# Block-sorted attention and a two-layer network on one core: a key load issued earlier, a product piece one slot earlier, and five products of zeros

## Chip, cores and metric

One core of a Trainium2 chip (trn2). The metric is the device time of the whole program in microseconds, lower is better. Each execution carries a state: "slow" ones (a few per cent longer, of any version: 237.31 us beside 233.39 to 233.86 in the first four runs of the kernel before) are left out of every comparison here unless the text says so.

## The reference, cut to what matters

```python
# q, k, v: (4 batches, 8 heads, 768 positions, 64); sort_net: (4, 8, 8, 8)
P = sort_net                                    # five rounds of exp, row and column normalisation
k_sorted = einsum('bhij,bhjcd->bhicd', P, k_b)  # blocks of 96 positions mixed by P
v_sorted = einsum('bhij,bhjcd->bhicd', P, v_b)
attn = softmax(q_b @ k_sb.T / 8)                # within each block
x = (attn @ v_sb), heads side by side           # (3072, 512)
h = x @ w_in                                    # (3072, 2048)
out = (s * relu(h)**2 + b) @ w_out              # (3072, 512)
```

## The kernel before

The work is cut into eight half batches, t = 0 to 7. The dense network of one half batch (`ffn1`, `ffn2`) carries pieces of the next attention between its products, through a queue of slots. Four places matter here.

The pieces that mix keys and values with P. Their results go to tiles in PSUM and are copied from there (`ks<-tk`, 0.42 to 0.81 us each at the start, on VectorE or ScalarE). A key piece multiplies 128 neighbouring numbers of `kb` as weights; a v piece of batch 0 takes its weights one number in 64:

```python
def k_piece(b, c0, nc2, nb, eng):
    ...                                          # ps: a PSUM tile, psa (3 buffers) or psb (2)
    for c in range(nc2):
        nc.tensor.matmul(out=ps[:, c, :],
                         lhsT=kb[pr, c0 + 2*c:c0 + 2*c + 2, :].rearrange("p c d -> p (c d)"),
                         rhs=rhs, start=True, stop=True)
    ...                                          # four copies to ks, on VectorE or ScalarE
def v_piece0(d0, n, eng):
    for t in range(n):
        nc.tensor.matmul(out=ps[:, t, :], lhsT=vb[0:64, :, d0 + t], rhs=..., start=True, stop=True)
    evac(VS[0][:, :, d0:d0 + n], ps[0:BLK].rearrange("p t g -> p g t"), eng)
```

The start, in TensorE's order. `warm_up` is a run of products of zeros, put there for the clock alone. In the profile of before each of them takes 421 ns at first and 272 from about 6.3 us on; what the eight later ones are worth is measured under no_pwarm:

```python
warm_up(76)
build_pd1()
q_half(0, "s")
k_piece(0, 0, 16, 1, "v")();  k_piece(0, 32, 16, 1, "s")()
k_piece(0, 64, 8, 1, "v")();  k_piece(0, 80, 8, 1, "s")()
v_piece0(0, 16, "v");  v_piece0(16, 16, "s");  v_piece0(32, 16, "v")
s_piece(0, 0);  v_piece0(48, 8, "v");  s_piece(0, 1);  v_piece0(56, 8, "v")
s_piece(0, 2);  s_piece(0, 3)
for hp in range(NHP):
    p_piece(0, hp, 0, 2)
    ...
    warm_up(2, psa)
```

GpSimd's queue, which issues the loads and also sums w_out for the bias, and the queue of pieces in which batch 2's keys are first used (K key pieces, V2 v pieces, S2 scores, P2 attention products, T transposes, `nothing` an empty slot):

```python
csums(0, 8)
v_read(1, nc.sync)            # batch 1's v comes back from DRAM, where v_piece1 wrote it
ffn1(1, ...)
load_v(*brows(3))
csums(8, NF)
qu = Queue([..., seq(lambda: load_q(2), lambda: load_k(*brows(2)), bias_piece),
            V2[0], S2(2, 0), ..., V2[5],
            seq(T(2), S2(3, 0), K(2, 0, 16, "s")), nothing, P2(3, 0),
            seq(S2(3, 2), K(2, 32, 16, "s")), nothing, P2(3, 2), ...], 24)
ffn2(0, qu); ffn2(1, qu)
```

The softmax here doesn't subtract the row's maximum and nothing guards it: scores larger than these inputs give would overflow.

Of the kernel before, what the change touches and what calls it, by code (L numbers as in the profile page):

```python
# [18 lines left out]
def kernel(  # L19
# [12 lines left out]
    nc = tc.nc  # L32
# [45 lines left out]
    def load_q(b, part=slice(0, 128)):  # L78


        if b > 1:
            qr[b] = qrp.tile([128, TQ, H, D], BF, tag="qr", name=f"qr{b}")
            for t in range(TQ):
                nc.gpsimd.dma_start(  # L84
                    out=qr[b][:, t],
                    in_=q[b][:, t * 128:(t + 1) * 128, :].rearrange("h p d -> p h d"))
            return
        if b not in qr:
            qr[b] = qrp.tile([128, H, TQ, D], BF, tag="qr", name=f"qr{b}")
        nc.gpsimd.dma_start(  # L90
            out=qr[b][part].rearrange("p h t d -> p h (t d)"),
            in_=q[b].rearrange("h (p t) d -> p h (t d)", t=TQ)[part])

    def load_k(rows, prow, n=1):
        for c0 in range(0, BLK, BLK // n):
            cs = slice(c0, c0 + BLK // n)
            nc.gpsimd.dma_start(out=kb[prow, cs, :], in_=kraw[rows, cs, :])

    def load_v(rows, prow):
        nc.gpsimd.dma_start(out=vb[prow, 0:BLK, :], in_=vraw[rows])  # L100

    def brows(b):
        return slice(b * 64, (b + 1) * 64), slice((b % 2) * 64, (b % 2) * 64 + 64)
# [6 lines left out]
    zt = const.tile([128, 256], BF)  # L110
# [41 lines left out]
    for c0 in range(0, d_ff, FCH):  # L152
        w = const.tile([128, NHP, FCH], BF, name=f"wi{c0}")
        nc.gpsimd.dma_start(
            out=w, in_=moe_w_in.rearrange("(hp p) f -> p hp f", p=128)[:, :, c0:c0 + FCH])
# [5 lines left out]
    for f0 in range(0, NF, FW):  # L161
        w = const.tile([128, FW, d_model], BF, name=f"wo{f0}")
        nc.gpsimd.dma_start(
            out=w, in_=moe_w_out.rearrange("(f p) n -> p f n", p=128)[:, f0:f0 + FW, :])
# [8 lines left out]
    def wo_at(f):  # L173
        return wos[f // FW][:, f % FW, :]
# [61 lines left out]
    def evac(out, in_, eng):  # L236
        if eng == "v":
            nc.vector.tensor_copy(out=out, in_=in_)  # L238
        else:
            nc.scalar.copy(out=out, in_=in_)  # L240
# [38 lines left out]
            nc.sync.dma_start(out=QT[b][:, :, t * 128:(t + 1) * 128],  # L279
                              in_=qr[b][:, t].rearrange("p h d -> p (h d)"), transpose=True)  # L280

    def k_piece(b, c0, nc2, nb, eng):




        pr = brows(b)[1] if nb == 1 else slice(0, 128)
        rhs = (pd1[pr] if b < 2 else pd2[pr, b - 2]).rearrange("p e m i -> p (e m i)")
        if nc2 * nb > 8:
            ps = psa.tile([128, nc2, nb * 64], FP, tag="a", name="tk")  # L290
        else:
            ps = psb.tile([128, nc2, nb * 64], FP, tag="b", name="tk")
        for c in range(nc2):
            nc.tensor.matmul(out=ps[:, c, :],  # L294
                             lhsT=kb[pr, c0 + 2 * c:c0 + 2 * c + 2, :].rearrange("p c d -> p (c d)"),
                             rhs=rhs, start=True, stop=True)
        g0 = (b % 2) * 32

        def half(cp):
            if b == 0:  # L300
                cs = slice(c0 + cp, c0 + 2 * nc2, 2)
            else:
                cs = slice(cp * (BLK // 2) + c0 // 2, cp * (BLK // 2) + c0 // 2 + nc2)
            for e in range(2):
                evac(ks[e * 64:(e + 1) * 64, g0:g0 + nb * 32, cs].rearrange(
                         "p (b g) c -> p b g c", b=nb),
                     ps[cp * 64:(cp + 1) * 64].rearrange(
                         "p c (b e g) -> p e b g c", b=nb, e=2)[:, e], eng)

        half(0)  # L310
        return lambda: half(1)

    def v_piece0(d0, n, eng):

        if n > 8:
            ps = psa.tile([128, n, 64], FP, tag="a", name="tv")
        else:
            ps = psb.tile([128, n, 64], FP, tag="b", name="tv")
        for t in range(n):
            nc.tensor.matmul(out=ps[:, t, :], lhsT=vb[0:64, :, d0 + t],  # L320
                             rhs=pd1[0:64].rearrange("p e m i -> p (e m i)"),
                             start=True, stop=True)
        evac(VS[0][:, :, d0:d0 + n], ps[0:BLK].rearrange("p t g -> p g t"), eng)
# [42 lines left out]
    def s_piece(t, hp):  # L366

        b, half = divmod(t, 2)
        g0 = (b % 2) * 32 + hp * NB + half * HB
        sc = psa.tile([BLK, 2, 512], FP, tag="a", name="sc")  # L370
        for n in range(HB):
            for e in range(2):
                pr = slice(e * 64, (e + 1) * 64)
                q0 = (half * HB + n) * BLK
                nc.tensor.matmul(out=sc[:, e, n * BLK:(n + 1) * BLK], lhsT=ks[pr, g0 + n, :],  # L375
                                 rhs=QT[b][pr, hp, q0:q0 + BLK], start=True, stop=True)
        at = atp.tile([BLK, 2, TG], BF, tag="at", name="at")
        nc.scalar.activation(out=at, in_=sc[:, :, 0:TG], func=AF.Exp, scale=scale)  # L378
        AT[t, hp] = at

    def p_piece(t, hp, n0=0, nn=HB):

        b, half = divmod(t, 2)
        at = AT[t, hp]
        if t not in X:
            X[t] = xp.tile([BLK, HB, d_model], BF, tag="x", name="x")
        x = X[t]
        atf = at.rearrange("p e t -> p (e t)")
        if nn < HB:
            p1 = psb.tile([128, 512], FP, tag="b", name="pv")  # L390
            pv = [p1[:, e * nn * VW:(e + 1) * nn * VW] for e in range(2)]
            pvv = p1[0:BLK, 0:2 * nn * VW].rearrange("p (e n w) -> p e n w", e=2, w=VW)
        else:
            p2 = psa.tile([128, 2, 512], FP, tag="a", name="pv")
            pv = [p2[:, 0], p2[:, 1]]
            pvv = p2[0:BLK, :, 0:nn * VW].rearrange("p e (n w) -> p e n w", w=VW)
        for e in range(2):
            for n in range(n0, n0 + nn):
                c0 = (e * HB + n) * BLK
                m = 128 if c0 + 128 <= 2 * TG else BLK  # L400
                gi = e * 32 + hp * NB + half * HB + n
                nc.tensor.matmul(out=pv[e][0:m, (n - n0) * VW:(n - n0 + 1) * VW],  # L402
                                 lhsT=atf[:, c0:c0 + m],
                                 rhs=VS[b][:, gi, :], start=True, stop=True)
        rec = rtp.tile([BLK, 2, HB], FP, tag="rec", name="rec")
        nc.vector.reciprocal(out=rec[:, :, 0:nn], in_=pvv[:, :, :, D])  # L406
        nc.vector.tensor_tensor(  # L407
            out=x[:, n0:n0 + nn, hp * 128:(hp + 1) * 128].rearrange("p n (e d) -> p e n d", e=2),
            in0=pvv[:, :, :, 0:D],
            in1=rec[:, :, 0:nn].unsqueeze(3).broadcast_to([BLK, 2, nn, D]), op=ALU.mult)  # L410
# [62 lines left out]
    def x_turn(t):  # L473

        XT[t] = xtp.tile([128, HB * NHP, BLK], BF, tag="xt", name="xt")
        nc.sync.dma_start(out=XT[t], in_=X[t].rearrange("p n m -> p (n m)"), transpose=True)
# [99 lines left out]
    def seq(*fs):  # L576
        def run():
            for f in fs:
                f()
        return run  # L580

    def S2(t, hp):
        return lambda: (s_piece(t, hp), s_piece(t, hp + 1))

    def P2(t, hp):
        return lambda: (p_piece(t, hp), p_piece(t, hp + 1))

    def T(t):
        return lambda: x_turn(t)
# [32 lines left out]
    build_pd1()  # L622
    q_half(0, "s")
    k_piece(0, 0, 16, 1, "v")()
    k_piece(0, 32, 16, 1, "s")()
    k_piece(0, 64, 8, 1, "v")()
    k_piece(0, 80, 8, 1, "s")()
    v_piece0(0, 16, "v")
    v_piece0(16, 16, "s")
    v_piece0(32, 16, "v")  # L630
    s_piece(0, 0)
    v_piece0(48, 8, "v")
# [36 lines left out]
    def csums(f0, f1):  # L669
        for f in range(f0, f1):  # L670
            if f == 1:
                nc.gpsimd.tensor_tensor(out=csum, in0=wo_at(0), in1=wo_at(1), op=ALU.add)
            elif f > 1:
                nc.gpsimd.tensor_tensor(out=csum, in0=csum, in1=wo_at(f), op=ALU.add)  # L674
# [2 lines left out]
    v_read(1, nc.sync)  # L677
    ffn1(1, Queue([nothing] * 4 + [build_pd2] + [nothing] * 3, 8))
    load_v(*brows(3))
    csums(8, NF)  # L680

    def K(b, c0, nc2, eng):
        return lambda: k_piece(b, c0, nc2, 1, eng)()
# [1 line left out]
    V2 = [lambda c0=c0: v_piece2(c0, "s") for c0 in range(0, BLK, 16)]  # L685
    qu = Queue([nothing, seq(lambda: q_piece(1, 2, "s"), K(1, 0, 16, "v")), nothing,
                seq(K(1, 32, 16, "s"), K(1, 64, 16, "v")), nothing,
                seq(lambda: load_q(2), lambda: load_k(*brows(2)), bias_piece),
                V2[0], S2(2, 0), V2[1], S2(2, 2), V2[2], V2[3], P2(2, 0), V2[4], P2(2, 2), V2[5],
                seq(T(2), S2(3, 0), K(2, 0, 16, "s")), nothing, P2(3, 0),  # L690
                seq(S2(3, 2), K(2, 32, 16, "s")), nothing, P2(3, 2),
                seq(T(3), lambda: q_turn(2)), K(2, 64, 16, "s")], 24)
    ffn2(0, qu)
# [56 lines left out]
```

## Time and profile before

| | before |
|---|---|
| time, median of 3 | 233.86 us (233.76 to 237.31) |
| span of the profiled run | 231.2 us |
| TensorE busy | 222.2 us, 96% |
| half clock in the profiled run | 16.56 to 26.80 us |
| first product of the first layer (hps) | 26.84 us |
| first score piece of t = 3 (sc) | 80.56 us |
| first product of the layer for t = 2 (hps) | 92.40 us |

The granted clock is the share of TensorE's full clock that the profile records; half clock is 0.50. It lasted 10.24 us in this profile and 13.65 in that of the changed kernel, three and four times 3.41; I call 3.41 us a window. In the profile, PE is TensorE's products, PEld its weight loads, DVE VectorE, ACT ScalarE, POOL GpSimd, SP SyncE; a q behind a name means its queue. Tiles: tk key pieces, tv v pieces, sc scores, at exponentials, pv attention products, hps first layer, ops second layer. A row of a timeline has start, length, engine, source line, operation, out<-in, shapes, count, and in brackets the engine's idle time before it with what ended it. The length runs to the modelled end of the last product, which matters below. The last three rows of the table are what I compare between versions: the distance from 80.56 to 92.40 is the middle, the 26.84 the start.

### The profile page before, as it was taken

How to read it: one execution, taken by the hardware profiler on the slowest of the kernel's cores; microseconds unless marked ns; L12 is line 12 of the kernel's file. 1: busy time of each engine (PE TensorE's matmuls, PEld its weight loads, DVE VectorE, ACT ScalarE, POOL GpSimd, SP SyncE). 2: the span in 40 equal slices, each digit the busy share in tenths (PEclk: the TensorE clock that was granted, in tenths of full speed). 3: DMA queues.
4: the chain of work that ended last, by engine and by line, in shares of the span. 5: the costliest groups of instructions: out<-in, count | busy, mean ns of one | idle time of the engine just before them, and what ended most of it. 6: DMA issues, size and time to landing. Idle time of an engine off the chain costs nothing.

```text
span 231.2 us, 4813 instructions
## 1 busy us (share of the span) xinstructions
PE 222.2 (96%) x2014; PEld 136.6 (59%) x2034; DVE 115.8 (50%) x244; ACT 115.9 (50%) x165; POOL 48.2 (21%) x62
## 2 busy tenths in 40 slices
PE   8989999999999979999999999999999999999994
PEld 5879887755644545565555555655555556654442
DVE  5778666738981625344445843343443634442221
ACT  6168479675468366866630285656222236660000
POOL 7820000399991000007911000000000000000000
PEclk9995699999999999999999999999999999999999
DMA  5999999999799991644999996610115240001212
GB/s 93 138 201 214 223 195 205 227 221 206 95 116 221 246 296 55 132 118 59 123 147 141 180 199 115 81 59 0 48 46 113 94 112 2 3 0 45 80 58 91
DMA packets 46694, 28.90 MB, mean 125 GB/s; under 512 B 35920, under 2 KB 41040, under 8 KB 46160
## 3 DMA queue, kind: packets, MB, share of 16 engines
q0 software_dynamic: 18800, 15.21, 46.6%
q1 hardware_dynamic: 27728, 13.32, 26.3%
q8 instruction: 16, 0.26, 0.5%
q10 hardware_dynamic: 144, 0.07, 0.1%
q14 instruction: 6, 0.05, 0.1%
HBM read 29.63 MB, written 8.65 MB: 166 GB/s over the span
## 4 chain that ended last, share of the span: by engine, by line
PE 91%; ACT 3%; DVE 3%; issue 1%; DVEq 0%
PE hps L498 36%; PE ops L552 34%; PE wp L182 5%; PE pv L402 4%; PE sc L375 3%; PE tk L294 2%; PE tv L320 2%; PE ops L537 2%; ACT ks L240 1%; DVE x L407 1%; PE tv L350 1%; PE tq L254 1%; ACT at L378 1%; ACT qt L240 1%; ACT rt L513 1%
## 5 line engine op out<-in xcount | busy, mean ns | idle before, releaser
L498 PE MATMUL hps<-xt,wi 128*128 128x384 bf16 (+1 forms) x576 | 87.0, 308 | 0.3
L552 PE MATMUL ops<-wo,gt 128*128 128x512 bf16 x348 | 82.9, 379 | 1.1 <-issue 0.2
L498 PEld LDWEIGHTS <-wi 128*128 128x128 bf16 x576 | 53.7, 98 | 30.6 <-issue 1.1
L513 ACT ACTIVATE rt<-hps 128x768 bf16<-128x768 f32 (+1 forms) x72 | 53.1, 741 | 37.0 <-PE hps L498 36.1
L514 DVE TENSOR_TENSOR gt<-rt 128x768 bf16<-128x768 bf16 (+1 forms) x72 | 41.7, 581 | 49.5 <-ACT rt L513 49.3
L552 PEld LDWEIGHTS <-gt 128*128 128x128 bf16 x368 | 34.1, 98 | 37.8 <-issue 0.6
L378 ACT ACTIVATE at<-sc 96x768 bf16<-96x768 f32 x32 | 24.4, 804 | 31.0 <-PE sc L375 30.8
L526 DVE SCALAR_TENSOR_TENSOR ot<-ops,s_bc,bias 128x512 f32<-128x512 f32 x23 | 17.2, 749 | 40.2 <-PE ops L552 40.1
L407 DVE TENSOR_TENSOR x<-pv,rec 96x512 bf16<-96x512 f32 (+1 forms) x36 | 22.6, 628 | 1.3
L240 ACT CAST ks<-tk 64x512 bf16<-64x512 f32 (+1 forms) x32 | 18.6, 582 | 5.3 <-PE tk L294 5.0
L674 POOL TENSOR_TENSOR csum<-csum,wo 128x512 f32<-128x512 f32 x14 | 17.6, 1255 | 1.0
L182 PE MATMUL wp<-zt 128*128 128x256 bf16 x84 | 13.5, 328 | 1.1 <-DVE warm L113 1.1
L402 PEld LDWEIGHTS <-at 96*128 96x128 bf16 (+1 forms) x256 | 12.0, 104 | 3.8
L238 DVE CAST ks<-tk 64x512 bf16<-64x512 f32 (+1 forms) x20 | 13.1, 654 | 2.1 <-PE tk L294 1.8
L402 PE MATMUL pv<-vs,at 96*128 96x66 bf16 (+1 forms) x256 | 13.0, 199 | 0.1
L240 ACT CAST vn<-tv 128x512 bf16<-128x512 f32 (+1 forms) x12 | 9.4, 799 | 6.4 <-PE tv L350 3.8
L406 DVE RECIPROCAL rec<-pv 96x8 f32<-96x8 f32 (+1 forms) x36 | 6.9, 193 | 10.9 <-PE pv L402 10.9
L84 POOL DMA_DIRECT2D qr<-in_q_dram x12 | 10.6, 910 | 5.3 <-DMA kb<-in_k_dram 3.1
L375 PEld LDWEIGHTS <-ks 64*96 64x96 bf16 x256 | 8.3, 128 | 5.7 <-issue 4.7
L182 PEld LDWEIGHTS <-zt 128*128 128x128 bf16 x84 | 9.4, 117 | 3.2 <-DVE warm L113 1.1
L375 PE MATMUL sc<-qt,ks 64*96 64x96 bf16 x256 | 10.7, 219 | 0.0
L294 PE MATMUL tk<-pd,kb 64*128 64x64 bf16 x192 | 7.1, 190 | 1.7 <-ACT at L378 1.4
(72 smaller groups left out, 96.2 us busy)
## 6 DMA issues: line engine op xcount, KB each, us to landing
out_dram<-ot SPq DMA_DIRECT2D x23, 256.0 KB, 2.6
kb<-in_k_dram POOLq DMA_DIRECT2D x4, 768.0 KB, 12.7
vb<-in_v_dram POOLq DMA_DIRECT2D x4, 768.0 KB, 18.7
wi<-in_moe_w_in_dram POOLq DMA_DIRECT2D x2, 1024.0 KB, 19.4
wo<-in_moe_w_out_dram POOLq DMA_DIRECT2D x2, 1024.0 KB, 32.0
qr<-in_q_dram POOLq DMA_DIRECT2D x12, 128.0 KB, 13.7
dv<-vn SPq DMA_DIRECT2D x6, 256.0 KB, 7.7
vs<-dv POOLq DMA_DIRECT2D x4, 384.0 KB, 13.1
```

The lines of the kernel that those rows point to most:

```text
L182: nc.tensor.matmul(out=wp, lhsT=zt[:, 0:128], rhs=zt, start=True, stop=True)
L240: nc.scalar.copy(out=out, in_=in_)
L375: nc.tensor.matmul(out=sc[:, e, n * BLK:(n + 1) * BLK], lhsT=ks[pr, g0 + n, :], rhs=QT[b][pr, hp, q0:q0 + BLK], start=True, stop=True)
L378: nc.scalar.activation(out=at, in_=sc[:, :, 0:TG], func=AF.Exp, scale=scale)
L402: nc.tensor.matmul(out=pv[e][0:m, (n - n0) * VW:(n - n0 + 1) * VW], lhsT=atf[:, c0:c0 + m], rhs=VS[b][:, gi, :], start=True, stop=True)
L407: nc.vector.tensor_tensor(out=x[:, n0:n0 + nn, hp * 128:(hp + 1) * 128].rearrange("p n (e d) -> p e n d", e=2), in0=pvv[:, :, :, 0:D], in1 ...
L498: nc.tensor.matmul(out=hps[:, f, 0:nt], lhsT=wi_at(hp, f0 + f), rhs=xt_at(t, hp, n0, nn), start=(hp == 0), stop=(hp == NHP - 1))
L513: nc.scalar.activation(out=rt[:, :, 0:nt], in_=hps[:, :, 0:nt], func=AF.Relu)
L514: nc.vector.tensor_tensor(out=gt[:, f0:f0 + 2, c0:c0 + nt], in0=rt[:, :, 0:nt], in1=rt[:, :, 0:nt], op=ALU.mult)
L526: nc.vector.scalar_tensor_tensor(out=ot, in0=ops, scalar=s_bc, in1=bias, op0=ALU.mult, op1=ALU.add)
L552: nc.tensor.matmul(out=ops, lhsT=gt[:, f, m * 128:(m + 1) * 128], rhs=wo_at(f), start=(f == 0), stop=(f == NF - 1))
L674: nc.gpsimd.tensor_tensor(out=csum, in0=csum, in1=wo_at(f), op=ALU.add)
```

## The change

The intent: have batch 2's keys in place before TensorE wants them, have a PSUM buffer freed before the next key piece wants it, and keep TensorE's clock up while the first pieces wait for copies and loads.

```diff
+    def zeros_to(out, n):
+        for _ in range(n):
+            nc.tensor.matmul(out=out, lhsT=zt[:, 0:128], rhs=zt, start=True, stop=True)
     # k_piece and v_piece0 get zeros=0 and call zeros_to(first 256 columns of ps, zeros) first
-    k_piece(0, 32, 16, 1, "s")()
-    k_piece(0, 64, 8, 1, "v")()
-    k_piece(0, 80, 8, 1, "s")()
-    v_piece0(0, 16, "v")
+    k_piece(0, 32, 16, 1, "s", 1)()
+    k_piece(0, 64, 8, 1, "v", 1)()
+    k_piece(0, 80, 8, 1, "s", 1)()
+    v_piece0(0, 16, "v", 2)
 ...
     load_v(*brows(3))
+    load_k(*brows(2))
     csums(8, NF)
 ...
-                seq(lambda: load_q(2), lambda: load_k(*brows(2)), bias_piece),
+                seq(lambda: load_q(2), bias_piece),
 ...
-                seq(T(2), S2(3, 0), K(2, 0, 16, "s")), nothing, P2(3, 0),
+                seq(T(2), S2(3, 0), K(2, 0, 16, "s")), P2(3, 0), nothing,
```

More of the change, by code (lines that the diff above doesn't have):

```diff
@@ L280, in q_turn, with k_piece @@
                               in_=qr[b][:, t].rearrange("p h d -> p (h d)"), transpose=True)
-    def k_piece(b, c0, nc2, nb, eng):
+    def zeros_to(out, n):
+        for _ in range(n):
+            nc.tensor.matmul(out=out, lhsT=zt[:, 0:128], rhs=zt, start=True, stop=True)
+    def k_piece(b, c0, nc2, nb, eng, zeros=0):
         pr = brows(b)[1] if nb == 1 else slice(0, 128)
@@ L292, in k_piece @@
             ps = psb.tile([128, nc2, nb * 64], FP, tag="b", name="tk")
+        zeros_to(ps[:, 0:4, :].rearrange("p c g -> p (c g)"), zeros)
         for c in range(nc2):
@@ L311, in k_piece, with v_piece0 @@
         return lambda: half(1)
-    def v_piece0(d0, n, eng):
+    def v_piece0(d0, n, eng, zeros=0):
         if n > 8:
@@ L318, in v_piece0 @@
             ps = psb.tile([128, n, 64], FP, tag="b", name="tv")
+        zeros_to(ps[:, 0:4, :].rearrange("p t g -> p (t g)"), zeros)
         for t in range(n):
```

## The prediction

> **What bounds the kernel now.** I read the page's busy line and slices first, then the chain of waits in order of time, then TensorE's timeline in the two places the change touches.
>
> The page, busy time by engine and the granted clock in 40 slices:
> ```profile
> PE 222.2 (96%) x2014; PEld 136.6 (59%) x2034; DVE 115.8 (50%) x244; ACT 115.9 (50%) x165; POOL 48.2 (21%) x62
> ...
> PEclk9995699999999999999999999999999999999999
> ...
> PE 91%; ACT 3%; DVE 3%; issue 1%; DVEq 0%
> ```
> TensorE (PE) is busy 222.2 of 231.2 us and 91% of the chain. So only two things are left: the 9.0 us in which it is idle, and stretches in which "busy" hides a slow clock. Slices 4 and 5 are such a stretch. The view by stretches, cut every 3.41 us (columns: window, length, busy us and count of PE, weight loads, DVE, ACT, POOL, then granted clock, DMA share, GB/s):
> ```profile
> 9.74:13.15 3.41, 3.41 (x70) 2.92 (x70) 2.06 (x11) 0.26 (x1) 2.01 (x3) 1.00 1.27 230
> 13.15:16.56 3.41, 2.28 (x69) 2.17 (x61) 2.65 (x5) 3.15 (x5) 0.66 (x2) 1.00 1.02 181
> 16.56:19.98 3.42, 3.17 (x37) 3.12 (x37) 3.30 (x6) 3.31 (x7) 0.20 (x1) 0.50 1.15 211
> 19.98:23.39 3.41, 3.41 (x58) 3.38 (x57) 2.59 (x4) 2.44 (x4) 0.25 (x1) 0.50 1.12 213
> 23.39:26.80 3.41, 3.31 (x34) 2.63 (x32) 2.58 (x9) 1.84 (x3) 0.29 (x1) 0.50 1.18 224
> 26.80:30.22 3.42, 3.33 (x47) 2.99 (x45) 2.04 (x8) 1.47 (x3) 0.00 (x0) 1.00 1.02 207
> 81.42:84.83 3.41, 2.33 (x25) 1.34 (x26) 0.00 (x0) 2.69 (x5) 0.00 (x0) 1.00 1.24 365
> ```
> The clock halves at 16.56 and comes back at 26.80, 10.24 us later[...]:
> ```profile
> 12.40 0.94 PE L254 MATMUL tq<-ident,qr 64*64 64x64 bf16 x48
> 13.38 1.56 PE L294 MATMUL tk<-pd,kb 64*128 64x64 bf16 x48
> 16.03 1.61 PE L320 MATMUL tv<-pd,vb 64*128 64x64 bf16 x16 [1.10 <-issue]
> ```
> The key pieces (tk) end at 14.94, and PE idles 1.10 us until the first v piece (tv). The load of batch 0's v was issued at 2.68 and took 13.3 us to land, so at 16.0: that is the wait, though the profile has no name for it.
>
> The second place, timeline at 69 to 83 us:
> ```profile
> 69.75 0.59 POOL L97 DMA_DIRECT2D kb<-in_k_dram  x1
> ...
> 80.98 1.50 ACT L378 ACTIVATE at<-sc 96x768 bf16<-96x768 f32 x2 [0.17 <-PE sc L375]
> ...
> 82.50 0.64 PE L294 MATMUL tk<-pd,kb 64*128 64x64 bf16 x16 [1.38 <-ACT at L378]
> ...
> 87.16 0.64 PE L294 MATMUL tk<-pd,kb 64*128 64x64 bf16 x16 [0.30 <-DVE x L407]
> ```
> PE idles 1.38 us before batch 2's first key piece. The profile names the exponentials (at), which end at 82.48. I choose another cause. The view of tile kb gives this load 12.7 us from issue to landing: 69.75 + 12.7 = 82.45. The PSUM buffer is no cause: with three buffers in turn, this piece takes the one of the last v piece, whose copy ended at 80.81. The 0.30 us at 87.16 is a buffer wait: that piece needs the PSUM buffer of the second product piece, which DVE empties (x) at 87.12.
>
> [...] at 69.7 us the key load starts behind six q loads, and slices 3 to 10 of the page move 195 to 227 GB/s while the early loads land one after the other. [...] In the trace the squares (gt) take 1.0 to 1.4 us while GpSimd sums w_out, against a mean of 0.58. The sums are only moved by one issue, so I give this no time.
>
> **Part 1: the key load ahead of the sums.** It goes from 69.75 to about 53.9, straight behind the v load at 53.38. That one needed 6.7 us to land and the DMA share is 0.3 to 0.4 between 58 and 62 us, so the keys land by about 61 to 66, over 15 us before they are used. Its target rows held batch 0's keys, read last at 15 us. Gain: 1.38 us of PE idle, on the path. Cost: one issue of 0.59 us on GpSimd before the eight last sums, which end at 64.54; the bias product that reads them begins at 65.26. Slack 0.72 against 0.59: hidden, with 0.13 left. The q loads also follow 0.59 later, but are not used before 93 us.
>
> **Part 2: one slot earlier for batch 3's half of the products.** P2(3,0) moves ahead by four w_out products (0.86 us). I walk PE with no key wait: key piece 81.1 to 81.7, four products to 82.55, pv to 83.1. Its exponentials end at 82.48, just in time. DVE empties pv at about 83.1 to 84.9; the next eight products end at 84.8, the two scores at 85.3, and the next key piece finds its buffer free. Gain 0.30. A possible new wait: those scores need the buffer that ACT empties from 82.5 over 4 x 0.58, to 84.85, so up to 0.1 us. Parts 1 and 2 together: 1.38 + 0.30 - 0.05 = **1.63 us**. From 92.4 on PE is full and its inputs (transposed x, then batch 2's q) are triggered from the same chain, so the gain is carried to the end.
>
> **Part 3: the products of zeros.** Five of 128*128 by 256 columns. The warm-up runs 76 of them in 10.98 us, and by its start-to-start at full clock [...] one takes 0.11 us. All five run before 16.03: three inside the key pieces, two in the idle of 1.10 us. PE ends them at about 15.5, ACT and DVE have a backlog until 19, so they cost nothing.
>
> What they buy: [...] I give it 6 in 10, since somebody placed exactly these five.
>
> Even if kept, the next window (16.56 to 19.98) holds little more than the remaining 37 tv products[...], so I expect **the half clock only to move to 19.97**, not to vanish. It then lasts until 23.4 or 26.8. What one full-clock window gives: the 32 tv products at 17.89, 2.96 us at half, take about 1.0, but the first scores need their PSUM buffer, emptied by DVE at 20.24, instead of starting at 20.71. About 0.45 us there, about 0.6 at the first pv (23.62 to 23.0). From there DVE paces: 0.18 + 0.42 us per piece, 0.65 apart.
>
> Then comes a cap. The second half of w_in is issued at 7.96 and lands 22.0 us later, at 29.96; its first product runs at 30.39. [...] So the start can gain at most about **0.4 us**; more turns into a wait of PE for this load. Expected: 0.6 x 0.4 = 0.25.
>
> **Sum.** 1.63 + 0.25 = 1.9; 233.86 - 1.9 = **231.9 us** (0.8%).
>
> **Rivals.**
> - The profile is right and the 1.38 us is a wait for the exponentials. For it: the release 0.02 us after they end. Against: neither data nor buffer of this piece depends on them. Then only the start gains, about 233.4. I give 1 in 10.
> - The zeros fail and the clock halves at 16.56 as before: 232.2.
> - The zeros hold the clock right through to 26.8: the start would be ahead by 1.2 to 1.5 us at 27.4, but the w_in load takes all but 0.4 back: 231.8. If that load came earlier too, 230.7.
> - The load on GpSimd delays the sums and the bias product becomes a wait: at most 0.59, so 232.5. The slack speaks against it.
> - The earlier key load slows the batch 1 v read (60.43, landing within 10.1 us at 70.5, used at 75.08): 4.5 us of slack speak against it.
>
> **Range and chances.** The rivals span 230.7 to 233.4. I take 230.8 to 233.0. A gain of over 2% needs 4.7 us; PE's whole idle time is 9.0, of which 1.13 are before the first product and 3.3 after the last, and part 3 is capped. Over 2% slower needs a new wait that nothing shows. Chances 0.03, 0.96, 0.01.
>
> **What would show it.** Key load at about 53.5 on GpSimd, landed before 67; no idle before the first key piece of batch 2 (about 80.7 to 81), none before the second. The bias product directly behind a w_out product. Clock 1.00 in 13.15:16.56 and 16.56:19.98, 0.50 after. The first product with w_in's second half not before 29.95, with PE idle in front. The prediction is wrong if the idle at 81 us stays, if the key piece's time reappears later in 84 to 92 us, or if the start gains more than 0.4 us at 30.4.

## The result

| | before | changed |
|---|---|---|
| median of 4 runs | 233.81 us (233.39 to 237.31) | 231.47 us (231.10 to 231.80) |
| span of the profiled run | 231.2 us | 230.1 us |
| half clock in the profiled run | 16.56 to 26.80 us | 14.01 to 27.66 us |
| first product of the first layer | 26.84 us | 27.77 us |
| sc of t = 3 to hps of t = 2 | 80.56 to 92.40: 11.84 us | 81.44 to 91.25: 9.81 us |

The ratio is 0.9905, with a 95% interval of 0.9877 to 0.9934. Ratios here are the mean time of one version's fast runs over the mean of the other's fast runs of the same rounds, so not quite the ratio of the medians. Inside the 2% band it counts as the same; it is 2.2 us faster.

The profiled run does not show these 2.2 us in one piece. It lost 0.93 us at the start and won 2.03 us in the middle. First the page of the changed kernel, the same three lines as before:

```profile
PE 223.0 (97%) x2019; PEld 137.1 (60%) x2039; DVE 116.1 (50%) x244; ACT 115.9 (50%) x165; POOL 48.5 (21%) x62
...
PEclk9975599999999999999999999999999999999999
...
PE 92%; DVE 4%; issue 1%; ACT 1%; DMA 1%
```

The low clock begins in slice 3, earlier than before, not later. The view by stretches, cut where this run's clock changes (busy us of PE, weight loads, DVE, ACT, POOL, then clock, DMA share, GB/s):

```profile
10.60:14.01 3.41, 2.31 (x70) 1.78 (x67) 1.80 (x9) 0.69 (x1) 1.48 (x2) 1.00 1.22 243
14.01:17.42 3.41, 3.41 (x39) 2.26 (x38) 3.33 (x6) 3.08 (x6) 0.54 (x1) 0.50 1.08 180
...
24.25:27.66 3.41, 3.30 (x34) 2.62 (x33) 2.65 (x9) 1.85 (x3) 0.35 (x1) 0.50 1.19 233
27.66:31.07 3.41, 3.35 (x48) 3.04 (x46) 1.99 (x8) 1.52 (x4) 0.00 (x0) 1.00 0.99 193
```

Four windows of half clock, and the whole pattern lies elsewhere: before, the products of the warm-up shorten from 421 to 272 ns at about 6.3 us and the clock falls at 16.56; here they do so at about 3.8, and it falls at 14.01, in both three windows later. TensorE's timeline at the start of the changed kernel (L284 are the new products of zeros):

```profile
13.27 0.62 PE L299 MATMUL tk<-pd,kb 64*128 64x64 bf16 x16
13.83 0.28 PE L284 MATMUL tk<-zt 128*128 128x256 bf16 x1
14.04 1.03 PE L299 MATMUL tk<-pd,kb 64*128 64x64 bf16 x16
15.01 0.39 PE L284 MATMUL tk<-zt 128*128 128x256 bf16 x1
...
16.74 0.61 PE L284 MATMUL tv<-zt 128*128 128x256 bf16 x2
17.28 4.39 PE L326 MATMUL tv<-pd,vb 64*128 64x64 bf16 x47
```

All but the first of the zeros run at half clock, and the first v piece starts at 17.28 instead of 16.03. In the middle, the same view, before first, its two ends (the key pieces between them are in the prediction), then the changed kernel:

```profile
80.56 0.56 PE L375 MATMUL sc<-qt,ks 64*96 64x96 bf16 x16
...
92.40 1.31 PE L498 MATMUL hps<-xt,wi 128*128 128x384 bf16 x7
```

```profile
81.44 0.56 PE L381 MATMUL sc<-qt,ks 64*96 64x96 bf16 x16
81.83 0.63 PE L299 MATMUL tk<-pd,kb 64*128 64x64 bf16 x16
...
86.02 0.63 PE L299 MATMUL tk<-pd,kb 64*128 64x64 bf16 x16
...
91.25 2.45 PE L504 MATMUL hps<-xt,wi 128*128 128x384 bf16 x14
```

Both key pieces of the changed kernel follow at once, without brackets. From sc to the first key piece it was 1.94 us and is 0.39; between the two key pieces it was 4.66 and is 4.19.

So the questions for the chip were: do the load and the slot make the middle, each its own part? What are the zeros worth, and why did the clock fall at another time?

### The profile page after: what moved, and what is told of

The parts are those of the page before. It is cut to its first block, busy times and chain, and to the rows that moved or that the text cites. A ratio compares the mean times of both kernels' runs of the same rounds, so it can differ in the third digit from the quotient of the medians.

```text
span 230.1 us, 4822 instructions
## 1 busy us (share of the span) xinstructions
PE 223.0 (97%) x2019; PEld 137.1 (60%) x2039; DVE 116.1 (50%) x244; ACT 115.9 (50%) x165; POOL 48.5 (21%) x62
## 4 chain that ended last, share of the span: by engine, by line
PE 92%; DVE 4%; issue 1%; ACT 1%; DMA 1%
PE hps L504 36%; PE ops L558 35%; PE pv L408 4%; PE sc L381 3%; PE tk L299 3%; PE tv L326 2%; PE ops L543 2%; PE tv L356 1%; PE tq L254 1%; PE tv L342 1%; PE wp L182 1%; PE tq L269 1%; DMA sn<-in_sort_net_dram 1%; DVE rstat L203 1%; ACT sn L197 1%
## 5 line engine op out<-in xcount | busy, mean ns | idle before, releaser
L558 PE MATMUL ops<-wo,gt 128*128 128x512 bf16 x348 | 82.9, 379 | 1.1 <-issue 0.2
L182 PE MATMUL wp<-zt 128*128 128x256 bf16 x84 | 12.2, 308 | 1.1 <-DVE warm L113 1.1
L182 PEld LDWEIGHTS <-zt 128*128 128x128 bf16 x84 | 8.8, 110 | 2.6 <-DVE warm L113 1.1
L240 ACT COPY qt<-tq 128x768 bf16<-128x768 bf16 (+1 forms) x6 | 5.9, 1014 | 5.1 <-PE tq L254 3.4
```

What stands on the lines that cost most here:

```text
L182: nc.tensor.matmul(out=wp, lhsT=zt[:, 0:128], rhs=zt, start=True, stop=True)
L240: nc.scalar.copy(out=out, in_=in_)
L558: nc.tensor.matmul(out=ops, lhsT=gt[:, f, m * 128:(m + 1) * 128], rhs=wo_at(f), start=(f == 0), stop=(f == NF - 1))
```

## The experiments

Twelve runs in three calls, each call on one chip, every kernel with five rounds beside the kernel before. All passed the comparison with the reference, even v_contig, which computes wrong values for batch 0 on purpose: the comparison's tolerance does not see them.

**My theory:** the middle is the landing of the key load (about 1.5 us) plus a buffer wait (about 0.5), both independent of the zeros; the zeros are worth little, and how little depends on when the clock falls (16.56 us in one profile, 14.01 in the other). **Rivals:** the wait in the middle is for the exponentials, as the profile had named it; the zeros make a good part of the gain; they only cost.

### before_copy: the kernel before, unchanged

> The kernel before, unchanged, to see the granted clock of every one of its runs. Theory A (the clock window starts at another moment in each execution): the half-clock stretch differs between runs by whole windows of 3.41 us (mean clock 0.985, 0.978 or 0.968), and runs with one window less are shorter by 0.3 to 0.9 us; ratio to before 1.000 within 0.002. Theory B (the window is fixed to the program): all runs show 0.978, and the same span within 0.1 us.

Measured: ratio 0.9989 (0.9957 to 1.0022). Its profiled run has half clock from 14.21 to 27.87, four windows, where the first profile of the same program had three from 16.56. Theory A holds: the window is not fixed to the program. Over the three calls the kernel before ran 33 times: 31 fast runs, of which 17 have a mean clock of 0.977 or 0.978 (mean time 232.88 us) and 14 have 0.968 to 0.971 (233.33 us). So the lottery of the window is worth about 0.45 us, within what I had allowed (0.3 to 0.9); the runs of either group scatter by about 0.6 us, which leaves it uncertain by some 0.4. None showed 0.985.

This run also speaks against the first rival: here the exponentials end at 82.81, 0.10 us before the piece starts (0.02 in the first profile), and the load, issued at 70.1, lands 12.8 us later, at 82.9:

```profile
80.89 0.56 PE L375 MATMUL sc<-qt,ks 64*96 64x96 bf16 x16
82.91 0.64 PE L294 MATMUL tk<-pd,kb 64*128 64x64 bf16 x16 [1.47 <-DMA kb<-in_k_dram]
```

The same wait as in the first profile, now put down to the DMA.

### load_only: the earlier key load alone

```diff
     load_v(*brows(3))
+    load_k(*brows(2))
     csums(8, NF)
-    seq(lambda: load_q(2), lambda: load_k(*brows(2)), bias_piece),
+    seq(lambda: load_q(2), bias_piece),
```

> Only the earlier key load. Mine: the idle time ahead of batch 2's first key piece was the landing of this load, so it goes, and the sc-to-tk distance falls from 1.94 us to about 0.4: 1.4 to 1.55 us faster, ratio about 0.9935; the 0.30 us buffer wait ahead of the second key piece stays or moves. Rival (the profile's name for it, the exponentials): the piece still begins when the second exponential ends, about 1.9 us after the first score product; ratio 1.000.

Measured: ratio 0.9948 (0.9919 to 0.9978), 232.01 against 233.17 us in the means. TensorE's timeline:

```profile
75.68 0.71 PE L402 MATMUL pv<-vs,at 96*128 96x66 bf16 x16 [0.28 <-DMA vs<-dv]
...
81.57 0.63 PE L294 MATMUL tk<-pd,kb 64*128 64x64 bf16 x16
...
86.23 0.64 PE L294 MATMUL tk<-pd,kb 64*128 64x64 bf16 x16 [0.28 <-DVE x L407]
```

The first wait is gone and the second stays, as expected; from sc to hps it takes 10.29 us, 1.55 less than before. The first line was not expected: the read of batch 1's v now comes 0.28 us too late. That is taken up under k_after_sums.

### swap_only: the earlier product slot alone

```diff
-    seq(T(2), S2(3, 0), K(2, 0, 16, "s")), nothing, P2(3, 0),
+    seq(T(2), S2(3, 0), K(2, 0, 16, "s")), P2(3, 0), nothing,
```

> Only the earlier product slot, the key load as before. Mine: the two waits are independent: the wait for the landing stays at 1.3 to 1.5 us, the 0.30 us buffer wait of the second key piece goes; 0.47 us faster, ratio 0.998. Rival (the swap pays only once the load is early): ratio 1.000 and the 0.3 us wait still there.

Measured: ratio 0.9969 (0.9940 to 0.9998), 0.74 us in the means; sc to hps takes 10.98 us, 0.86 less. This run also settles the first rival. The exponentials (`at`) end at 82.48 again, and the key piece no longer comes after them:

```profile
80.98 1.50 ACT L378 ACTIVATE at<-sc 96x768 bf16<-96x768 f32 x2 [0.16 <-PE sc L375]
82.12 0.64 PE L294 MATMUL tk<-pd,kb 64*128 64x64 bf16 x16 [1.00 <-DMA kb<-in_k_dram]
```

It starts 0.36 us before they end, as its load lands.

The second wait is gone: 4.20 us between the key pieces (82.12 to 86.32), 0.46 less. The remaining 0.4 us is the first wait, 1.00 us here: this load landed 12.3 us after 69.7, in the profile of before 12.7. The two parts are independent.

### load_swap, load_swap_b, load_swap_c: both, without the zeros

The two diffs above together, in each of the three calls.

> The earlier key load and the earlier product slot, no products of zeros. Mine: 2.0 us faster (1.55 and 0.47 read from the traces of before and after), ratio 0.991, and from the start of batch 1's first layer to 92 us the same timeline as the changed kernel, shifted. Rival (the zeros carry a good part of the gain): only 1.5 us or less, ratio 0.9935 or more.

> load_swap again, as the partner of after_copy: ratio to before 0.991 within 0.002, span 229.2 to 229.5 whatever the clock.

> load_swap once more, as the partner of the other three: ratio 0.991 to 0.992.

Measured: 0.9908 (0.9878 to 0.9937), 0.9919 (0.9889 to 0.9950), 0.9921 (0.9899 to 0.9942): 231.06, 231.24 and 231.03 us in the means, some 1.9 to 2.1 us faster. From sc to hps it is 9.81 us in the fast profiles, exactly the changed kernel's; load_swap's:

```profile
80.67 0.56 PE L375 MATMUL sc<-qt,ks 64*96 64x96 bf16 x16
...
90.48 3.26 PE L498 MATMUL hps<-xt,wi 128*128 128x384 bf16 x19
```

The whole gain of the changed kernel is there without a product of zeros. Two of eight runs of load_swap_b were slow, its profile among them.

### zeros_only: the five products of zeros alone

> Only the five products of zeros. Mine: 0 to 0.4 us faster on average, ratio 0.998 to 1.000, depending on how many windows of half clock each run has; where the window falls as in the profile of before, the half clock starts one window later. Rival (they hold the clock in every run): mean clock 0.985 or more in all runs and 0.4 us or more faster, ratio 0.998 or less. Second rival (they only cost): slower by up to 0.5 us, ratio 1.002.

Measured: ratio 1.0008 (0.9978 to 1.0037). In its profiled run the clock falls at 16.89, near the 16.56 of before, so it tests what the prediction expected of the zeros:

```profile
13.48:16.89 3.41, 3.38 (x63) 2.63 (x60) 2.66 (x5) 3.30 (x5) 0.64 (x2) 1.00 1.05 180
16.89:20.31 3.42, 3.42 (x41) 3.42 (x40) 3.30 (x6) 3.31 (x7) 0.00 (x0) 0.50 1.15 214
```

All five zeros fell into the window that ends at 16.89, PE counts as busy for 3.38 of its 3.41 us, and the clock fell all the same. The profile of before has a window that kept the clock with PE busy for 2.33 us (81.42 to 84.83) and one that lost it with 2.28 (13.15 to 16.56), so the busy time does not tell which will; what does, these runs do not show. The first layer starts at 27.05, just as in load_only, which has no added zeros and the same mean clock (0.978): the zeros neither gain nor cost there.

The timed runs leave one thing open. One of the six here has a mean clock of 0.984 (232.99 us) and one of the changed kernel's first four 0.985 (231.10 us), a window of half clock less. That is 2 of 16 runs with the five zeros, against none of 82 fast runs without added zeros. So the zeros may hold the clock for a window now and then; no trace of such a run was kept. Both were only 0.02 and 0.05 us faster than the next run of their version.

### after_copy: the changed kernel, beside load_swap_b

> The changed kernel itself, beside load_swap (the same without the five zeros) on one chip. Mine, after zeros_only: the zeros buy nothing; runs in which the clock falls near 14 us pay for zeros at half clock. after_copy 229.4 to 230.1 us of span, load_swap_b 229.2 to 229.5; so after_copy is 0.0 to 0.5 us slower, ratio to before 0.990 to 0.993 against 0.991. Rival (the zeros help in the whole): after_copy faster than load_swap_b by 0.3 us or more.

Measured: ratio 0.9940 (0.9913 to 0.9967), 231.70 against 231.24 us for load_swap_b. The intervals overlap, so the 0.46 us is an indication; the profiles show where it may come from. The clock fell at 14.31 here and the first layer starts at 27.66. Against the kernel before in the same phase (before_copy: clock down at 14.21, first layer at 27.02, first v piece at 16.18), the changed kernel's two profiles (down at 14.01 and 14.31) start the layer at 27.77 and 27.66, 0.64 to 0.75 us later. In these two profiles, where the window falls early, the zeros run at half clock on the path and cost; in that of zeros_only, where it falls late, they cost nothing and still don't hold the clock.

### hold_late: enough zeros to hold the clock

load_swap, with the last 10 of the 76 warm-up products made to wait for a copy at 10.5 us, and zeros ahead of the v pieces:

```diff
-    warm_up(76)
+    warm_up(66)
+    warm_late(10)                 # read a tile of zeros that ScalarE writes after the fifth exp
-    v_piece0(0, 16, "v")
+    v_piece0(0, 16, "v", 18)
-    v_piece0(32, 16, "v")
+    v_piece0(32, 16, "v", 10)
     # and 3 each ahead of v_piece0(48, ...) and v_piece0(56, ...)
```

> load_swap with 18 zeros ahead of the first v piece, 10 ahead of the third, 3 ahead of each of the last two, and the last 10 warm-up products bound to a copy at 10.4 us so that an early full clock does not end the warm-up early. Made to hold the clock from 10 to 23 us. Mine: in most runs the clock stays full up to about 20 us or beyond (mean clock 0.985 or more); the first layer starts 0.5 to 1.0 us earlier than in load_swap (26.9), and then TensorE waits for the second half of w_in, landing at 29.9 to 30.1, so that no more than 0.4 to 0.5 us is left at its first product: ratio to before 0.989 to 0.991. Rival 1 (the start is set by ScalarE's and VectorE's copies, not by the clock): first layer no more than 0.3 us earlier even at full clock. Rival 2 (no cap by the load): 0.8 us or more gained on load_swap.

Measured: ratio 1.0104 (1.0066 to 1.0143), slower; my expectation failed. The clock did hold, up to 19.98, and fell there, so that the later zeros ran at half clock and the first layer began at 32.00. But it gave what I needed most: the same v pieces at full clock. First hold_late, clock 1.00 up to 19.98, then the weight loads of those products in hold_late and, from the profile of before, at half clock (min/median/max ns):

```profile
17.16 3.10 PE L333 MATMUL tv<-pd,vb 64*128 64x64 bf16 x32
...
L333 PEld LDWEIGHTS <-vb x32: 165/215/242, 17.2 to 19.9; 64*128 64x128 bf16 x32
```

```profile
L320 PEld LDWEIGHTS <-vb x31: 168/202/215, 17.9 to 20.5; 64*128 64x128 bf16 x31
```

The 32 products take 3.10 us at full clock and 2.96 at half. Less the last one's own length, that is (3.10 - 0.25) / 31 = 92 ns from start to start at full clock and (2.96 - 0.27) / 31 = 87 at half. The clock is worth nothing to them. Their weight load takes over 200 ns at either clock (medians of 215 and 202); that this is what bounds them, the next run tests. The trace of before could have said it: its first six v products run ahead of the fall at 16.56, and (0.70 - 0.27) / 5 = 86 ns.

```profile
16.03 0.70 PE L320 MATMUL tv<-pd,vb 64*128 64x64 bf16 x6 [1.10 <-issue]
```

### v_contig: the same products with neighbouring weights

```diff
-    lhsT=vb[0:64, :, d0 + t],
+    lhsT=vb[0:64, d0 + t:d0 + t + 2, :].rearrange("p c d -> p (c d)"),   # wrong values on purpose
```

> load_swap with the weights of the first v pieces read as 128 neighbouring columns instead of one in 64; the result is wrong on purpose. Mine: the tv products at 92 to 97 ns apart at both clocks are bound by that weight load, so here they run 60 to 65 ns apart at half clock and about 32 at full, as the key pieces do; 32 of them take 2.0 us instead of 2.96 and the first layer starts 0.3 to 0.6 us earlier than in load_swap (26.9), ratio 0.989 to 0.990. Rival (a product of 64 columns from 64 rows costs what it costs): spacing 92 ns or more, no change.

The profiled run counts as slow, so its time is not compared, only its start, where it is undisturbed; load_swap_b's profile, slow as well, has a median of 211 ns for these loads at half clock and starts the first layer at 26.95, so the slow state does not make the difference below. Weight loads of the v pieces, most of them at full clock (to 16.58), then at half:

```profile
L320 PEld LDWEIGHTS <-vb x21: 92/95/129, 16.1 to 18.0; 64*128 64x128 bf16 x21
```

```profile
L320 PEld LDWEIGHTS <-vb x22: 125/129/129, 17.9 to 19.0; 64*128 64x128 bf16 x22
```

The load falls from 202 to 129 ns at half clock. The 16 products of the first piece, at full clock, take 0.64 us, and the 32 at half clock 1.86: 30 and 52 ns from start to start. Now the clock matters, and the spacing is what I had assumed for the real kernel. The first layer starts at 26.35, 0.6 to 0.8 us earlier than in load_swap's fast profiles (26.94, 27.17). The rival is out.

The time did not follow: 0.9943 (0.9912 to 0.9975), five fast runs spread from 230.54 to 232.32. In the profiled run the product at 76.79 waits 1.99 us for the read of batch 1's v. Whether the fast runs lose the start's gain to the same read, I did not see.

### k_after_sums: the key load between the sums and the q loads

```diff
     load_v(*brows(3))
-    load_k(*brows(2))
     csums(8, NF)
-    seq(lambda: load_q(2), bias_piece),
+    seq(lambda: load_k(*brows(2)), lambda: load_q(2), bias_piece),
```

> load_swap with the key load behind the sums but ahead of the six q loads (at about 64.5 us instead of 54). Mine: the key load at 54 us pushes the write and read of batch 1's v (read issued at 60.4 to 61.0 before, at 62.0 to 66.0 with the early load) and eats the slack ahead of the first product of batch 1's second half; at 64.5 us it should land by about 75, still ahead of 80.5, so 2.0 us are kept, ratio 0.991, and the v read is issued at 60.4 to 61.0 again. Rival (64.5 is too late): the wait ahead of the first key piece is back, 0.3 us or more, ratio 0.993 or more.

Measured: ratio 0.9922 (0.9899 to 0.9945), 231.11 us against 231.03 for load_swap_c; no wait ahead of either key piece, sc to hps again 9.81 us. The read of batch 1's v in SyncE's queue, first the changed kernel, then k_after_sums:

```profile
64.42 2.33 SPq L367 DMA_DIRECT2D vs<-dv  x2
```

```profile
60.91 2.92 SPq L361 DMA_DIRECT2D vs<-dv  x2
```

The issue had been at 60.43 before. With the key load at 54 us, the last write of v to DRAM lands later (9.0 us after its issue at 55.2 in the changed kernel, 6.0 after 54.3 before), and the read that waits for it moves to 62.0 to 64.4 in the fast profiles. In before its second half was issued at 60.8 and landed 10.1 us later, at 70.9, 4.2 us ahead of its use at 75.08. In load_only it landed 11.2 us after its issue just behind 64.07, and TensorE waited 0.28. A slow run shows how this goes on; in load_swap_b's profile the read was issued at 66.01 and

```profile
79.95 1.11 PE L402 MATMUL pv<-vs,at 96*128 96x66 bf16 x16 [4.53 <-DMA vs<-dv]
```

I do not compare that run with fast ones, and slow runs come with the kernel before as well (2 of 33). Whether the early load makes them more frequent, these runs do not show. With the key load at 64.9, landing 9.2 us later, the read keeps its slack and nothing is lost.

### no_pwarm: without the eight older products of zeros

```diff
     for hp in range(NHP):
         p_piece(0, hp, 0, 2)
         ...
-        warm_up(2, psa)
```

> load_swap without the eight older products of zeros between the first product pieces (23.6 to 26.5). Mine: the clock is worth time where dense products run, so without these zeros the half clock lasts one window longer, into the first layer, whose first products then take about 1.3 us per group of eight instead of 0.66: 0.5 to 1.5 us slower than load_swap, mean clock 0.963 to 0.970. Rival (the clock at the start is worth nothing anywhere): equal or faster, since eight products of 0.21 us are gone.

Measured: ratio 0.9964 (0.9939 to 0.9989), 232.05 against 231.03 us for load_swap_c. The first groups of the first layer, no_pwarm first, then load_swap_c:

```profile
26.59 1.46 PE L498 MATMUL hps<-xt,wi 128*128 128x192 bf16 x8
...
28.11 1.13 PE L498 MATMUL hps<-xt,wi 128*128 128x192 bf16 x8
```

```profile
27.17 1.11 PE L498 MATMUL hps<-xt,wi 128*128 128x192 bf16 x8
...
28.26 0.83 PE L498 MATMUL hps<-xt,wi 128*128 128x192 bf16 x8
```

It starts the layer 0.58 us earlier and has lost that, and 0.15 more, by the group at 30.91 (30.76 in load_swap_c), since its half clock lasts until 28.76 (27.47 there) and these products feel it: 1.13 us for the group at 28.11, 0.83 for the one at 28.26 there. All six runs have a mean clock of 0.963 or 0.970, load_swap_c's six 0.975 to 0.978. The profiled pair differs by 0.4 us of span; of these, 0.25 come later, at 75.83, where the attention product starts as the read of batch 1's v lands (issued at 63.5, 12.3 us). The means differ by 1.0; how much of that is the clock's, no trace shows. So the clock is worth time at the start, but at the first layer (0.73 us in this pair), not at the v pieces.

### The version to keep

load_swap and k_after_sums are at least as fast as the changed kernel (231.03 to 231.24 us against 231.46 and 231.70, partly on other chips) and lack the zeros; k_after_sums also keeps the slack of the v read. I would keep k_after_sums.

## Why the prediction was right, step by step

- **The middle, predicted 1.63 us: the mechanism right, the size too small.** The traces give 2.03 us (11.84 to 9.81): 1.55 for the load, 0.48 for the slot. I had used the idle times 1.38 and 0.30. They run from the modelled end of the product before, and that end lies behind the moment at which the next product can start: in the changed kernel the first tk starts 0.39 us after the first sc, while the sc row alone is 0.56 long. Each wait was worth 0.17 us more than its idle time. My allowance of 0.05 for a new wait wasn't needed.
- **The cause of the 1.38 us.** I chose the landing against the profile's name. Right: load_only removes the wait, before_copy's profile names the DMA, and in swap_only the piece starts before the exponentials end.
- **Sums and bias product.** Hidden, as worked out: the bias product is at 66.14 in the changed kernel, 0.88 later than before, the same as the whole timeline there (sc at 81.44 against 80.56).
- **The v read.** I dismissed this rival with 4.5 us of slack. That counted the landing from the first issue, at 60.43; the later half was issued at 60.8, so it was 4.2. Right for the time of the changed kernel, where 1.5 us are left (landing 9.7 us after 64.8, used at 75.95), but in load_only the slack is gone and TensorE waits 0.28 us.
- **The zeros, predicted 0.25 us: wrong in three steps.** "I give it 6 in 10", an estimate, that the zeros hold the clock for one more window: in none of the three profiles with them do they, once with all five in the window and PE busy for 3.38 of 3.41 us (zeros_only); in 2 of 16 runs they may have. "All five run before 16.03", "so they cost nothing": only where the window falls late; I had taken one profile's window for the program's, and in both profiles of the changed kernel four of the five run at half clock. And the step that mattered most, "the 32 tv products at 17.89, 2.96 us at half, take about 1.0": they take 3.10 us at full clock (hold_late), because one-in-64 weights bound them (with neighbouring ones, in v_contig, products at full clock come 30 ns apart instead of 92). So the 0.45 us that I took from these products was not to be had. What a full clock would buy in the scores behind them, no run shows, since hold_late's fell at 19.98. Measured for the zeros: 1.0008 alone, and 0.46 us slower in after_copy than in load_swap_b, with overlapping intervals.
- **The cap by w_in's second half** was never reached, since the start gained nothing. It stays untested, and its 0.4 us took one profile's landing for all: in before_copy, with the same issue, the load lands at 28.7 instead of 29.96.
- **The sum.** 231.9 predicted (233.86 less 1.63 and 0.25 is 231.98, rounded down), 231.47 measured. The middle gave 0.4 us more and the start at least 0.25 less. That these two errors have opposite signs is luck; what is left between the 2.03 us of the middle and the 2.3 between the medians lies within the interval of the ratio. In the copies' rounds the changed kernel stood at 231.76.

## What to carry to other kernels

Before buying a faster clock for a stretch, divide the length of its products by their count and ask whether the clock or the weight load sets the spacing: 92 ns at full clock and 87 at half say it at once. An idle time ends at the start of the waiting product but begins at a modelled end (1.38 us of it were worth 1.55 here); measure what a wait is worth from start to start. And a load moved earlier can move into someone else's transfer (in load_only it turned the v read's 4.2 us of slack into a wait of 0.28): look up the slack of every DMA it now runs beside, and move it only as far as it needs.
